# Three edits to the background schedule of an attention + two-MoE-layer kernel on one core: wider spacing of dependent pieces, rounded weights kept in their raw-word buffer, another rhythm for attention

## The chip, the core and the metric

One core of a Trainium2 chip runs the whole program. The metric is device time in microseconds (us) of one launch, measured for whole executions. A profile is one further execution, taken by the hardware profiler; its own time and span stand in the table below.

## What is computed

```python
# windowed attention: 4 x 8 heads, 768 positions, 64 wide; chunks of 32 with 16 left, 8 right, 8 memory slots
scores = scale * np.matmul(q_c, k_full.transpose(0, 1, 3, 2))
a = np.exp(scores - np.max(scores, axis=-1, keepdims=True))
a = a / (np.sum(a, axis=-1, keepdims=True) + 1e-09)
out[:, :, c_start:c_end] = np.matmul(a, v_full)
# x: 3072 tokens x 512; two dense "MoE" layers, 512 -> 2048 -> 512
h = x @ w_in;  r = np.maximum(h, 0.0);  x = (r * r) @ w_out            # first layer
h = x @ w_in;  g = h * np.tanh(softplus(h));  out = g @ w_out          # second layer
```

The four weight matrices arrive as 64-bit floats. The kernel decodes them on the chip into 32-bit floats.

## The kernel before

**Steps and points.** The two layers are worked in 48 steps: layer, then one of three token blocks of 1024 tokens (`sb`), then one of eight slices of d_ff (`j`). Layer 1 is steps 0 to 23, layer 2 steps 24 to 47. In a step PE does seven block products of a Strassen-Winograd scheme for the first matmul of that step (`product`, L527), and, between them, the second matmul of the step before (`unit`, L582, eight units). Each product or unit ends with a call of `rest()`, and that call is a *point*: 15 points in a step, numbered 0 to 14. A full step without attention is 90 matmuls of 128x512.

**What is hung on the points.** `beside` holds, by step and point, everything that is not the main chain: `at(s, i, work)` puts it there, and `rest()` does it. In order of program each point first flushes stores and raw loads that were put off by `later`, then streams one or two weight pieces (`stream_w`, L259: `w1s` for the next step, and in steps 8 to 23 `w2s` for the units of the next step, at points 1, 4, 7 and 10), then does the hung work. Each engine runs its instructions in the order in which they were written, and so does SP, which issues every DMA of this kernel.

**Weights.** `order_w` lists 32 weight blocks (layer, slice, which matrix). For each, `plan_w(s, i, e, order, ...)` hangs nine pieces from point `i` of step `s` on, one letter each; `|` goes on by a point. `A` (ACT, L155) rebuilds the high word into `val`, `D` (DVE, L160 and L163) clips and shifts it, `d` (DVE, L169) joins the low word, `S` and `s` (DVE, L180 to L185) make sums, `R` and `r` (ACT, L207 or L225) round the first and the second part to the fp32r format of the matmuls, `L` and `l` (DVE, L213 or L232) take what the rounding left. The 64-bit words lie in `raws`, two slots used in turn; `load_raw(n + 2)` refills a slot for the block after next. Layer 1's blocks are decoded in steps 0 to 7, two a step; layer 2's 16 blocks one a step in steps 8 to 14 and then one every 10 points from step 17 on. Layer 2's parts are stored to DRAM (`w_d`) and streamed back later.

**Attention.** Group `p` (0 to 11) is 256 tokens by 8 heads. Groups 0 to 3 are done ahead of step 0; groups 4 to 7 are hung from step 0 on and 8 to 11 from step 8 on, by `plan_attention`: scores on PE (L375), maxima on DVE, 16 exponentials on ACT (L411), normalisation (L421, L425), transposes (L433), a copy (`pt`, L443), the product with v (L455), a copy to `stage` (L467), sums on GpSimd, a store. PSUM banks 6 and 7 serve scores, transposes and values of all these groups in turn. `v` of a group shares its buffer (`at1`) with `stage` of the one before, `q` shares `xt0` with the probabilities, and `load_x` reuses `xt0` to `xt2` and `at0`, `at1` in steps 7 and 15 to fetch the next token block, which `split_x` (L287, L289) rounds.

Of the kernel before, what the change touches and what calls it, by code (L numbers as in the profile page):

```python
# [29 lines left out]
NQ = KF // 2  # L30
# [28 lines left out]
def tile_chunk_attention_moe_moe2(  # L59
# [105 lines left out]
    def decode(e):  # L165
        n = order_w.index(e)
        vb = val_t[e][:, 0:1024].bitcast(U32).rearrange("p (h f) -> p h f", h=2)
        low = raw_of(n).bitcast(U32).rearrange("p h (f b) -> p h f b", b=2)[:, :, :, 0]
        nc.vector.scalar_tensor_tensor(  # L169
            out=vb, in0=low, scalar=29, in1=vb, op0=ALU.logical_shift_right, op1=ALU.bitwise_or  # L170
        )
        load_raw(n + 2)

    def sums_w(e, half):

# [41 lines left out]
            del val_t[e]  # L217
            later((w1_d, w2_d)[kind][0][j], w.bitcast(FP32))

    def round_w2(e, i, tag):  # L220

        v0, o, n = parts(e)[i]
        flush()
        hi_t[e, i] = pool.tile([128, 1024], FP32R, tag=tag, name="hi")
        nc.scalar.copy(out=hi_t[e, i][:, 0:n], in_=val_t[e][:, v0:v0 + n])  # L225

    def split_w2(e, i):
        _, j, kind = e
# [453 lines left out]
    def plan_attention(s, i, p):  # L682

        for n, work in {
            0: lambda: scores(p),
            1: lambda: softmax(p, 0),
            2: lambda: softmax(p, 1),
            3: lambda: (exps(p, 0, slice(0, 4)), load_k(p + 1) if (p + 1) % PSB else None),
            4: lambda: exps(p, 0, slice(4, 8)),
            5: lambda: exps(p, 1, slice(0, 4)),  # L690
            6: lambda: exps(p, 1, slice(4, 8)),
            7: lambda: normalize(p),
            8: lambda: load_v(p) if p > PSB else None,
            13: lambda: transpose_p(p),
            14: lambda: (copy_pt(p), load_q(p + 1) if (p + 1) % PSB else None),
            17: lambda: values(p),
            18: lambda: copy_x(p),
            19: lambda: sums_x(p, nc.gpsimd),
            24: lambda: store_x(p),
        }.items():  # L700
            at(s, i + n, work)

# [175 lines left out]
    with tc.manual_schedule():  # L878
# [85 lines left out]

        for s in range(NQ):
            if s + 1 < NQ:
                plan_w(s, 0, (0, s + 1, 0), "A||D|d|RS|s||rL||l", round_w, split_w, "val")
                plan_w(s, 5, (0, s, 1), "A||D|d||R||L", round_w, split_w, "xt2")
            else:
                plan_w(s, 5, (0, s, 1), "A||D|d||R||L", round_w, split_w, "val")  # L970

        seconds = [e for e in order_w if e[0]]
        for n, e in enumerate(seconds):
            if n < NQ - 1:
                plan_w(NQ + n, 3, e, "A||D|d|RS|s|L||||r|l", lambda e, i: round_w2(e, i, "xt2"), split_w2, "val")
            else:
                n -= NQ - 1
                hi = (["xt0", "xt1"], ["xt2", "at1"])[n % 2]
                plan_w(
                    2 * NQ + 1, 10 * n, e, "A||D|d|RS|s|Lr||l",  # L980
                    lambda e, i, hi=hi: round_w2(e, i, hi[i]), split_w2, ("val", "at0")[n % 2],
                )

        for sb in range(NSB - 1):
            p = PSB * (sb + 1)
            start, first, period = sb * NQ, 10, 22
            at(start, 0, lambda p=p: load_q(p))
            if sb:
                at(start, 1, lambda p=p: load_k(p))
# [106 lines left out]
```

## Time and profile before

| what | value |
|---|---|
| time, median of 3 runs (lowest, highest) | 1093.74 us (1091.49, 1094.07) |
| the profiled execution: its own time, its span | 1093.48 us, 1091.7 us |
| PE busy | 1047.6 us, 96% of the span |
| DVE, ACT, GpSimd busy | 76%, 53%, 39% |
| mean granted TensorE clock | 0.987 |
| DMA moved | 321.37 MB, mean 294 GB/s |

The span runs from the first to the last instruction; the time is 1.8 us longer. "PE" is the matmul row, "PEld" the weight loads that run beside it. In the rows further down, "<-" behind an idle time names what ended the wait, and L527 is a line of the kernel as printed above.

### The profile page before, as it was taken

The numbers are of one execution on the slowest core, as the hardware profiler recorded it, in microseconds if no ns is written. First come the engines' busy times: TensorE is split into PE (matmuls) and PEld (weight loads), VectorE is DVE, ScalarE is ACT, GpSimd is POOL, SyncE is SP. The second block draws the span as 40 slices with busy tenths as digits, with TensorE's granted clock in tenths as the row PEclk, the third lists the DMA queues.
The fourth block names the chain that finished last, engine by engine and source line by source line (L and its number), as shares of the span: only waits on it lengthen the run. The fifth ranks groups of instructions, "written<-read, shape, count | busy, mean of one in ns | idle before, by whom it ended". The sixth has DMA issues, their size and how long they took to land.

```text
span 1091.7 us, 19711 instructions
## 1 busy us (share of the span) xinstructions
PE 1047.6 (96%) x7443; PEld 847.9 (78%) x7443; DVE 831.3 (76%) x1027; ACT 583.2 (53%) x1087; POOL 426.5 (39%) x327
## 2 busy tenths in 40 slices
PE   6879999998989999999999999999999999999998
PEld 3557777776778888788888788888888888888887
DVE  5777868759847667778898767887868878867777
ACT  2567765746665764666565654444354443453332
POOL 2224253322324343222222244545455454644443
PEclk9899999999999999999999999999999999999999
DMA  9646867669999998989998988899998899987452
GB/s 352 265 147 252 326 248 267 245 250 345 339 350 342 344 316 289 305 299 361 369 331 318 316 295 283 307 329 320 387 356 279 297 310 360 377 264 228 157 174 77
DMA packets 192142, 321.37 MB, mean 294 GB/s; under 512 B 13488, under 2 KB 151088, under 8 KB 188208
## 3 DMA queue, kind: packets, MB, share of 16 engines
q1 hardware_dynamic: 192048, 320.11, 84.1%
q8 instruction: 60, 0.98, 0.4%
q14 instruction: 34, 0.28, 0.1%
HBM read 228.04 MB, written 92.01 MB: 293 GB/s over the span
## 4 chain that ended last, share of the span: by engine, by line
PE 70%; DVE 11%; DMA 10%; ACT 5%; issue 3%; SPq 1%; DVEq 0%; ACTq 0%
PE banks L527 32%; PE banks L617 20%; PE banks L582 13%; DMA w1s<-w_d 3%; DMA xt_d<-stage 2%; DMA xt<-xt_d 2%; PE banks L455 2%; DVE val L169 2%; DVE y L596 1%; DVE w1s L213 1%; PE banks L375 1%; PE banks L660 1%; ACT p L411 1%; DVE val L163 1%; ACT val L155 1%
## 5 line engine op out<-in xcount | busy, mean ns | idle before, releaser
L527 PE MATMUL banks<-x,w1s 128*128 128x512 f32 x2016 | 496.9, 393 | 12.7 <-DVE u L849 5.3
L527 PEld LDWEIGHTS banks<-x,w1s 128*128 128x128 f32 x2016 | 379.2, 189 | 97.2 <-DVE u L849 6.6
L541 POOL TENSOR_TENSOR g<-r,g 128x512 fp32r<-128x512 f32 x190 | 266.5, 1410 | 478.0 <-ACT g L540 380.3
L582 PE MATMUL banks<-g,w2s 128*128 128x512 f32 x1152 | 282.0, 395 | 7.8 <-DVE y L596 5.7
L582 PEld LDWEIGHTS banks<-g,w2s 128*128 128x128 f32 x1152 | 215.8, 189 | 59.5 <-DVE y L596 9.2
L617 PE MATMUL banks<-g,w2s 128*128 128x512 f32 x828 | 206.5, 389 | 0.0
L617 PEld LDWEIGHTS banks<-g,w2s 128*128 128x128 f32 x828 | 155.4, 188 | 32.4
L540 ACT CAST g<-r 128x512 fp32r<-128x512 f32 x190 | 116.0, 622 | 27.7 <-DVE r L568 23.3
L596 DVE TENSOR_TENSOR y<-banks,y 128x512 f32<-128x512 f32 x168 | 112.0, 680 | 21.4 <-PE banks L582 21.3
L605 DVE TENSOR_TENSOR m<-banks,m 128x1024 f32<-128x1024 f32 (+1 forms) x84 | 101.1, 1209 | 12.4 <-PE banks L617 7.2
L541 POOL TENSOR_TENSOR g<-raws,g 128x512 fp32r<-128x512 f32 x47 | 66.8, 1426 | 62.7 <-ACT g L540 37.2
L546 ACT ACTIVATE r<-r 128x512 f32<-128x512 f32 x72 | 45.5, 632 | 71.0 <-DVE r L857 49.7
L550 ACT ACTIVATE r<-r 128x512 f32<-128x512 f32 x48 | 30.4, 633 | 73.1 <-DVE r L857 37.3
L605 DVE TENSOR_TENSOR raws<-banks,raws 128x1024 f32<-128x1024 f32 x40 | 48.9, 1222 | 26.7 <-PE banks L617 26.7
L547 ACT ACTIVATE r<-r 128x512 f32<-128x512 f32 x96 | 60.9, 634 | 3.1
L232 DVE TENSOR_TENSOR val<-val,hi 128x1024 f32<-128x1024 f32 (+1 forms) x32 | 39.9, 1248 | 29.3 <-ACT hi L225 28.6
L830 DVE TENSOR_TENSOR u<-banks,u 128x512 f32<-128x512 f32 x48 | 32.9, 685 | 26.6 <-ACT u L823 21.8
L849 DVE TENSOR_TENSOR u<-banks,u 128x512 f32<-128x512 f32 x48 | 33.1, 689 | 22.8 <-PE banks L527 20.1
L823 ACT COPY u<-banks 128x512 f32<-128x512 f32 x48 | 28.5, 594 | 39.8 <-PE banks L527 39.7
L169 DVE SCALAR_TENSOR_TENSOR val<-raws,val 128x1024 uint32<-128x1024 uint32 x32 | 48.4, 1511 | 0.7
L425 POOL TENSOR_TENSOR p<-p,sum 128x512 f32<-128x512 f32 x22 | 27.7, 1278 | 52.6 <-DVE sum L422 22.2
L155 ACT ACTIVATE val<-raws 128x1024 f32<-128x1024 f32 x32 | 36.6, 1143 | 21.1 <-DMA w_d<-val 10.1
(96 smaller groups left out, 1078.8 us busy)
## 6 DMA issues: line engine op xcount, KB each, us to landing
w1s<-w_d SPq DMA_DIRECT2D x280, 256.0 KB, 6.0
w2s<-w_d SPq DMA_DIRECT2D x229, 256.0 KB, 6.0
raws<-w_dram SPq DMA_DIRECT2D x64, 512.0 KB, 5.2
w_d<-w1s SPq DMA_DIRECT2D x8, 1792.0 KB, 9.4
x<-xs_d SPq DMA_DIRECT2D x14, 1024.0 KB, 11.3
v<-v_dram SPq DMA_DIRECT2D x24, 512.0 KB, 7.7
xt<-xt_d SPq DMA_DIRECT2D x21, 512.0 KB, 7.7
k<-k_dram SPq DMA_DIRECT2D x24, 368.0 KB, 7.4
```

What stands on the lines that cost most here:

```text
L155: nc.scalar.activation(out=val, in_=high, func=ACTF.Prelu, scale=REBIAS, alpha=NEGATIVE)
L169: nc.vector.scalar_tensor_tensor(out=vb, in0=low, scalar=29, in1=vb, op0=ALU.logical_shift_right, op1=ALU.bitwise_or)
L232: nc.vector.tensor_tensor(out=val, in0=val, in1=hi, op=ALU.subtract)
L527: nc.tensor.matmul(out=ps, lhsT=w[:, a, f:f + 128], rhs=x[:, xi, c, kk, :], start=start and i == 0, stop=stop and i == len(order) - 1, ski ...
L540: nc.scalar.copy(out=g[:, 0], in_=r)
L541: nc.gpsimd.tensor_tensor(out=g[:, 1], in0=r, in1=g[:, 0].bitcast(FP32), op=ALU.subtract)
L546: nc.scalar.activation(out=r, in_=h, func=ACTF.Relu)
L547: nc.scalar.activation(out=r, in_=r, func=ACTF.Square)
L582: nc.tensor.matmul(out=ps, lhsT=w[:, a, blk(f), d % 2 * 128:d % 2 * 128 + 128], rhs=g_t[s, (f, t)][:, c, :], start=i == 0, stop=i == len(o ...
L596: nc.vector.tensor_tensor(out=y, in0=ps, in1=y, op=ALU.add)
L605: engine.tensor_tensor(out=to, in0=in0, in1=in1, op=ALU.add)
L617: nc.tensor.matmul(out=bank(first + d), lhsT=w[:, a, 128 * d:128 * d + 128], rhs=g[:, c, :], start=i == 0 and blk not in ONTO, stop=i == 2 ...
```

## The change

Three things. The order strings of `plan_w` put the pieces of one weight block at other points. For layer 2, the rounded part is no longer written to a buffer of its own (`xt2`, or `xt0`, `xt1`, `at1` in steps 17 on) but over the block's raw words in `raws`; so the refill of that slot can no longer be asked for when the words have been joined (`decode`), and is asked for behind the last store instead (`split_w2`). Attention's groups 4 to 7 begin at point 14 of step 0 instead of point 10, both sets of groups come every 20 points instead of 22, and from the transposes on each piece stands one point earlier in its group (the store two).

```diff
@@ decode
-        load_raw(n + 2)
+        if e[0] == 0:
+            load_raw(n + 2)
@@
-    def round_w2(e, i, tag):
+    def round_w2(e, i):
         v0, o, n = parts(e)[i]
-        flush()
-        hi_t[e, i] = pool.tile([128, 1024], FP32R, tag=tag, name="hi")
+        hi_t[e, i] = raw_of(order_w.index(e))[:, i].bitcast(FP32R)
         nc.scalar.copy(out=hi_t[e, i][:, 0:n], in_=val_t[e][:, v0:v0 + n])
@@ split_w2
         later(d[:, 0, o:o + n], hi)
         later(d[:, 1, o:o + n], val)
         if i == len(parts(e)) - 1:
             del val_t[e]
+            load_raw(order_w.index(e) + 2)
@@ plan_attention
-            13: lambda: transpose_p(p),
-            14: lambda: (copy_pt(p), load_q(p + 1) if (p + 1) % PSB else None),
-            17: lambda: values(p),
+            12: lambda: transpose_p(p),
+            13: lambda: (copy_pt(p), load_q(p + 1) if (p + 1) % PSB else None),
+            16: lambda: values(p),
...
@@ steps 0 to 7
-                plan_w(s, 0, (0, s + 1, 0), "A||D|d|RS|s||rL||l", round_w, split_w, "val")
-                plan_w(s, 5, (0, s, 1), "A||D|d||R||L", round_w, split_w, "xt2")
+                plan_w(s, 0, (0, s + 1, 0), "A||D|d||S|R|s|L|r||l", round_w, split_w, "val")
+                plan_w(s, 4, (0, s, 1), "A||D|||d|||R|||L", round_w, split_w, "xt2")
...
@@ steps 8 to 14, then from step 17
-                plan_w(NQ + n, 3, e, "A||D|d|RS|s|L||||r|l", lambda e, i: round_w2(e, i, "xt2"), split_w2, "val")
+                plan_w(NQ + n, 3, e, "A|D|d|S|Rs||Lr||l", round_w2, split_w2, "val")
...
-                    2 * NQ + 1, 10 * n, e, "A||D|d|RS|s|Lr||l",
+                plan_w(2 * NQ + 1, 10 * n, e, "A||D|d|S|Rs||Lr||l", round_w2, split_w2, ("val", "at0")[n % 2])
...
-            start, first, period = sb * NQ, 10, 22
+            start, first, period = sb * NQ, (14, 10)[sb], 20
```

Most line numbers of the kernel after (L173 to L221, and L238 to the plan at L979) are higher by one than here: its L260 is L259 here, its L850 is L849.

SP in step 19, points 6 to 10, before (`hi` is the rounded part, `val` what is left; what an instruction waits for stands in brackets, and `DMAHW` is a semaphore that counts landed DMAs):

```order
L136 DMA w_d<-hi 128x768 [waits DMAHW3_49,Activation_49]
L136 DMA w_d<-val 128x768 [waits DMAHW4_49,DVE_49]
L259 DMA w2s<-w_d 128x2x256 [waits DMAHW5_49]
L259 DMA w1s<-w_d 128x2x256 [waits DMAHW6_49]
L136 DMA w_d<-hi 128x1024 [waits DMAHW7_49,Activation_49]
L136 DMA w_d<-val 128x1024 [waits DMAHW0_49,DVE_49]
L259 DMA w1s<-w_d 128x2x256 [waits DMAHW1_49]
L259 DMA w2s<-w_d 128x2x256 [waits DMAHW2_49]
```

and the same place after:

```order
L136 DMA w_d<-raws 128x768 [waits DMAHW2_49,Activation_49]
L136 DMA w_d<-val 128x768 [waits DMAHW3_49,DVE_49]
L260 DMA w1s<-w_d 128x2x256 [waits DMAHW4_49]
L136 DMA w_d<-raws 128x1024 [waits DMAHW5_49,Activation_49]
L136 DMA w_d<-val 128x1024 [waits DMAHW6_49,DVE_49]
L136 DMA raws<-w_dram 128x1024 [waits DMAHW7_49,DMAHW2_49]
L136 DMA raws<-w_dram 128x1024 [waits DMAHW5_49,DMAHW0_49]
L260 DMA w1s<-w_d 128x2x256 [waits DMAHW1_49]
L260 DMA w2s<-w_d 128x2x256
```

Between the store of the second rounded part and the `w2s` piece of point 10 there now stand two refills of `raws`, and the second of them waits for DMAHW5, which is that store's own landing. It is so again in steps 17 and 21; elsewhere the refills come at other points.

DVE in step 2, around point 6 and 7, before (L849 makes `u` of the chain, which the product at point 10 waits for; the first L213 takes what rounding left of `w1s`):

```order
L185 TENSOR_TENSOR val<-val 128x256
L849 TENSOR_TENSOR u_1528<-banks,u_1380 128x512
L851 TENSOR_TENSOR r<-banks,u_1528 128x512
L213 TENSOR_TENSOR w1s<-val,w1s 128x768
L160 TENSOR_SCALAR val<-val 128x1024
L163 TENSOR_SCALAR val<-val 128x1024
L596 TENSOR_TENSOR y<-banks,y 128x512
L169 SCALAR_TENSOR_TENSOR val<-raws,val 128x1024
```

and after:

```order
L160 TENSOR_SCALAR val<-val 128x1024
L163 TENSOR_SCALAR val<-val 128x1024
L394 TENSOR_REDUCE mx<-banks 128x8
L401 TENSOR_SCALAR mneg<-mx 128x8
L850 TENSOR_TENSOR u_1518<-banks,u_1373 128x512
L852 TENSOR_TENSOR r<-banks,u_1518 128x512
L186 TENSOR_TENSOR val<-val 128x256
L597 TENSOR_TENSOR y<-banks,y 128x512
L214 TENSOR_TENSOR w1s<-val,w1s 128x768
```

The pair L160, L163 of the second weight block has moved ahead of L849, the sum L185 and the take-off L213 behind it.

ACT at the turn from step 0 to step 1, before (L823 copies the bank that the product of point 5 adds to; L411 are the exponentials of group 4):

```order
L411 ACTIVATE p,sum<-banks,mneg 128x64 x8
L155 ACTIVATE val<-raws 128x1024
L411 ACTIVATE p,sum<-banks,mneg 128x64 x4
L823 COPY u_1128<-banks 128x512
L411 ACTIVATE p,sum<-banks,mneg 128x64 x4
```

and after:

```order
L155 ACTIVATE val<-raws 128x1024
L824 COPY u_1109<-banks 128x512
L412 ACTIVATE p,sum<-banks,mneg 128x64 x8
L595 COPY y<-banks 128x512
L155 ACTIVATE val<-raws 128x1024
```

All exponentials of group 4 now stand behind that copy.

## Rows read from the trace of the kernel before

**Rows 1.** Busy time by stretch (windows): steps 0-7, 8-10, 11-15, 17-23; PEclk granted clock.

```profile
57.00:257.83 200.83, 182.93 (x1734) 145.98 (x1733) 151.95 (x202) 130.48 (x292) 68.46 (x54) 0.97 0.71 257
257.83:334.49 76.66, 70.86 (x667) 56.90 (x666) 55.50 (x78) 51.23 (x130) 23.96 (x20) 0.98 0.98 348
334.49:450.49 116.00, 115.58 (x1117) 94.84 (x1116) 79.58 (x111) 68.81 (x156) 44.26 (x36) 1.00 0.94 321
472.74:616.56 143.82, 143.31 (x632) 118.10 (x630) 123.24 (x162) 84.79 (x125) 38.01 (x27) 1.00 0.97 343
```

**Rows 2.** Waits of PE from 57 to 450 us: total, times, longest.

```profile
PE banks L527 <- DVE u L849: 5.3, 3, 3.3
PE banks L582 <- DVE y L596: 4.6, 6, 2.0
PE banks L527 <- ACT u L823: 4.4, 2, 3.1
PE banks L363 <- ACT stage L467: 3.0, 2, 2.8
PE banks L455 <- ACT val L155: 1.8, 1, 1.8
```

**Rows 3.** Waits of PE from 472 to 616 us.

```profile
PE banks L582 <- DMA w2s<-w_d: 0.4, 1, 0.4
```

**Rows 4.** Windows: a stretch at low granted clock, and step 19 whole.

```profile
83.90:87.30 3.40, 3.40 (x10) 2.61 (x9) 3.29 (x6) 1.54 (x5) 1.74 (x2) 0.50 0.71 284
514.20:534.60 20.40, 20.40 (x91) 16.89 (x90) 18.51 (x26) 14.81 (x22) 7.24 (x5) 1.00 1.00 361
```

**Rows 5.** Timeline of PE, steps 0 and 1: start, length, idle before.

```profile
66.22 1.66 PE L527 MATMUL banks<-x,w1s 128*128 128x512 f32 x6 [1.57 <-DVE u L849]
...
74.17 3.01 PE L527 MATMUL banks<-x,w1s 128*128 128x512 f32 x12 [1.93 <-DVE r L857]
...
82.97 1.29 PE L527 MATMUL banks<-x,w1s 128*128 128x512 f32 x4 [3.07 <-ACT u L823]
```

**Rows 6.** Timeline of DVE in step 0.

```profile
67.67 0.69 DVE L160 TENSOR_SCALAR val<-val 128x1024 f32<-128x1024 f32 x1
...
70.09 2.20 DVE L169 SCALAR_TENSOR_TENSOR val<-raws,val 128x1024 uint32<-128x1024 uint32 x1
72.21 1.21 DVE L213 TENSOR_TENSOR w1s<-val,w1s 128x1024 fp32r<-128x1024 f32 x1
```

**Rows 7.** Timeline of SP at the turn to step 7.

```profile
228.34 0.38 SPq L481 DMA_DIRECT2D xt_d<-stage  x1
...
239.98 1.21 SPq L273 DMA_DIRECT2D xt<-xt_d  x2
```

**Rows 8.** Timeline of ACT in step 7.

```profile
244.57 1.05 ACT L287 CAST x<-xt 128x1024 fp32r<-128x1024 f32 x1 [11.15 <-DMA xt<-xt_d]
```

**Rows 9.** Timeline of ACT in step 10.

```profile
312.99 1.05 ACT L225 CAST hi<-val 128x1024 fp32r<-128x1024 f32 x1 [3.68 <-DMA w_d<-hi]
313.94 1.06 ACT L467 COPY stage<-banks 128x512 f32<-128x512 f32 x2
```

**Rows 10.** Timeline of ACT in step 19.

```profile
528.76 0.62 ACT L540 CAST g<-r 128x512 fp32r<-128x512 f32 x1
```

**Rows 11.** Timeline of SP in step 19.

```profile
530.72 1.03 SPq L259 DMA_DIRECT2D w2s<-w_d  x1
```

**Rows 12.** Timeline of PE at point 3 of step 20.

```profile
538.68 1.52 PE L582 MATMUL banks<-g,w2s 128*128 128x512 f32 x6
```

**Rows 13.** Stores of `hi`, 472 to 600 us, from issue to landing.

```profile
DMA to landing us min/median/max: 2.6/6.1/8.0
```

**Rows 14.** Weight pieces (L259), 472.7 to 596 us, from issue to landing.

```profile
DMA to landing us min/median/max: 5.2/6.7/8.1
```

**Rows 15.** DMA issues of the whole run: size of one, median us to landing.

```profile
v<-v_dram SPq DMA_DIRECT2D x24, 512.0 KB, 7.7
...
w_d<-hi SPq DMA_DIRECT2D x17, 512.0 KB, 4.7
```

More of the change, by code (lines that the diff above doesn't have):

```diff
@@ L693, in plan_attention @@
             8: lambda: load_v(p) if p > PSB else None,
-            13: lambda: transpose_p(p),
-            14: lambda: (copy_pt(p), load_q(p + 1) if (p + 1) % PSB else None),
-            17: lambda: values(p),
-            18: lambda: copy_x(p),
-            19: lambda: sums_x(p, nc.gpsimd),
-            24: lambda: store_x(p),
+            12: lambda: transpose_p(p),
+            13: lambda: (copy_pt(p), load_q(p + 1) if (p + 1) % PSB else None),
+            16: lambda: values(p),
+            17: lambda: copy_x(p),
+            18: lambda: sums_x(p, nc.gpsimd),
+            22: lambda: store_x(p),
         }.items():
@@ L966, in tile_chunk_attention_moe_moe2 @@
             if s + 1 < NQ:
-                plan_w(s, 0, (0, s + 1, 0), "A||D|d|RS|s||rL||l", round_w, split_w, "val")
-                plan_w(s, 5, (0, s, 1), "A||D|d||R||L", round_w, split_w, "xt2")
+                plan_w(s, 0, (0, s + 1, 0), "A||D|d||S|R|s|L|r||l", round_w, split_w, "val")
+                plan_w(s, 4, (0, s, 1), "A||D|||d|||R|||L", round_w, split_w, "xt2")
             else:
-                plan_w(s, 5, (0, s, 1), "A||D|d||R||L", round_w, split_w, "val")
+                plan_w(s, 4, (0, s, 1), "A||D|||d|||R|||L", round_w, split_w, "val")
         seconds = [e for e in order_w if e[0]]
@@ L974, in tile_chunk_attention_moe_moe2 @@
             if n < NQ - 1:
-                plan_w(NQ + n, 3, e, "A||D|d|RS|s|L||||r|l", lambda e, i: round_w2(e, i, "xt2"), split_w2, "val")
+                plan_w(NQ + n, 3, e, "A|D|d|S|Rs||Lr||l", round_w2, split_w2, "val")
             else:
                 n -= NQ - 1
-                hi = (["xt0", "xt1"], ["xt2", "at1"])[n % 2]
-                plan_w(
-                    2 * NQ + 1, 10 * n, e, "A||D|d|RS|s|Lr||l",
-                    lambda e, i, hi=hi: round_w2(e, i, hi[i]), split_w2, ("val", "at0")[n % 2],
-                )
+                plan_w(2 * NQ + 1, 10 * n, e, "A||D|d|S|Rs||Lr||l", round_w2, split_w2, ("val", "at0")[n % 2])
         for sb in range(NSB - 1):
             p = PSB * (sb + 1)
-            start, first, period = sb * NQ, 10, 22
+            start, first, period = sb * NQ, (14, 10)[sb], 20
             at(start, 0, lambda p=p: load_q(p))
```

## The prediction

> **What bounds the kernel now.** I read the stage table first. PE does the work that ends last: it is busy for 96% of the span, and a full step without attention takes 20.40 us with PE busy in all of it [rows 4]. So time can only be won where PE waits or runs slowly, and the table says where. From step 11 to 15 PE lacks 0.4 us of 116.0, in steps 17 to 23 0.5 us of 143.8. In steps 0 to 7 it lacks 17.9 us of 200.8, in steps 8 to 10 5.8 us of 76.7 [rows 1]: 23.7 us together. The list of PE's waits says for whom: mostly DVE (`u`, `y`, `r`) and ACT (`u`, `stage`) [rows 2]. One of them, the 1.8 us put down to ACT `val`, was over for ACT's part, since that instruction stands behind the waiting one in the program; the load of `v` is what was late there.
>
> Second, the clock. A wait of 3.07 us [rows 5] is followed by 3.4 us at a granted clock of 0.50, which is 1.2 GHz [rows 4], and costs 1.7 us again. Waits of 1.57 and 1.93 us were not followed by one [rows 5]. There are five such stretches between 57 and 335 us, 8.5 us. With the idle time that is 32.2 us at most to win, all of it before 335 us.
>
> Third, the DMA queue. DMA is at a share of 0.98 in steps 8 to 10 and 0.97 in steps 17 to 23 [rows 1]. SP issues in order and waits itself: the load of `xt` at 239.98 stood for some 11 us after the store of 228.34, which writes what it reads, and held all that SP had behind it [rows 7]. The one DMA wait of PE in steps 17 to 23, 0.4 us, is for `w2s` [rows 3]: these pieces arrive with nothing to spare.
>
> **The change part by part.** The number of instructions and bytes is the same; all the cost is in waiting. My unit is the point, 20.40/15 = 1.36 us.
>
> *Steps 0 to 2.* The exponentials of group 4 now stand behind ACT's copy `u`, so the wait of 3.07 us goes and its slow stretch with it: 4.8 us. The wait of 1.93 us came from a join (2.20) and a take-off (1.21) on DVE just ahead of `r` [rows 5, 6]; these now stand elsewhere: 1.9 us. Against that, a pair of 0.69 each takes the place of a shorter sum ahead of L849 [rows 6], so the 1.57 becomes about 2.6: 1.0 lost. And three new waits: the second matmul of step 1 needs the `w2s` take-off, which moved from point 12 to point 0 of step 1, behind two activations and a cast; the transposes of group 4 need a normalisation behind a late GpSimd operation; the values at point 0 of step 2 need the copy `pt`, hung at point 12, ACT's fullest point. I put each at 1.2 to 1.5 us by adding ACT's durations from the end of step 0: 3.9 lost. Net gain 1.8.
>
> *Steps 3 to 6.* The wait for `v` (1.8 and a slow stretch) shrinks: the `w2s` store that shared the DMA engines with it is issued later. Gain 3.0. The waits for `y` [rows 2] in step 5, 2.4 us with a slow stretch, come from DVE's backlog after point 7, which the spacing spreads into points 6 and 0, where DVE had nothing: gain 3.6, less 1.0 for the values at point 0 of step 6. Net 2.6. If DVE stays behind there, both stay.
>
> *Step 7.* Group 7's store moves from point 10 to point 6 of step 6, 5.4 us earlier and ahead of the big weight store. The load of `xt` then needn't wait; it can land near 239 us, where the rounding of `x` began only at 244.57 [rows 7, 8]. PE's 3.3 us for `u` [rows 2], the following 0.8 and 1.2 us for `y` and the slow stretch, 7.0 us, shrink to about 1. Gain 6.0.
>
> *Steps 8 to 10.* The rounded part no longer shares one buffer for both halves, so ACT no longer stands 3.68 us for a landing ahead of the copies to `stage` [rows 9]. That was the longest wait of L363 [rows 2], 3.0 with its tail, plus a slow stretch. Gain 4.7.
>
> *Steps 10 to 14.* `q` and `v` of groups 10 and 11 are now issued just behind a refill of `raws` that waits for a store's landing, and 8 points ahead of use instead of 9. A load of `v` takes 7.7 us in the median [rows 15]; with the hold before it that is a point too late at three or four places: 3.5 lost. The bounds are 0 and 10 (each wait 2.5).
>
> Sum to here: 1.8 + 3.0 + 2.6 + 6.0 + 4.7 - 3.5 = 14.6 us won; bounds 5 (the new waits twice as long) and 25 (none of them).
>
> *Steps 17 to 22.* Here the refill stands directly ahead of the `w2s` piece of point 10 in steps 17, 19 and 21. Step 19 worked out: the second rounding follows the activation group that ended at 529.38 [rows 10] and takes 1.05; DVE frees that group 0.9 sooner, so the store goes at 529.5. It lands in 4.7 us (this size, whole run [rows 15]) to 6.1 (this stretch [rows 13]); I take 5.4: 534.9. Then the refill and a `w1s` piece are issued, 1.0 us, and the `w2s` piece goes at 535.9 instead of 530.72 [rows 11]. With 6.7 us [rows 14] it lands at 542.6. PE comes to it with its third matmul after 538.68 [rows 12], at 539.1. So PE waits 3.5 us, and by what the waits above did, a slow stretch follows, 1.7. Three times: 15.6 us lost. Nothing covers it: PE has 0.5 us to spare in the whole stretch [rows 1]. Bounds: 2.6 and 5.2 us [rows 13, 14] give no wait; 8.0 and 8.1 give 7.5 each, 27.6 in all.
>
> The Trainium skill, "DMA: Bandwidth & Descriptors", section "Anatomy of one DMA — SWDGE (gpsimd) path", gives 2.0 us plus the bytes at 436 GB/s for a DMA, a fit for the GpSimd path. By that, as an estimate, the store would take 3.2 us and the piece 2.6; the piece would land at 536.3, the loss would be zero and the time 1079. The trace has 4.7 to 6.7 us for these two [rows 13 to 15], on SP's queue with others in flight, so the page's price is not used; it speaks for the first rival.
>
> Sum: the profiled execution took 1093.48 us (the median of the three is 1093.74). 1093.5 - 14.6 + 15.6 = 1094.5. I say 1094.
>
> **The rivals.**
>
> *The holds stay hidden (0.26).* If the store lands within 3.5 us and the piece within 5.2, it arrives at 539.2, when PE comes. For it: with SP held, less is in flight than in the rows. Against: the pieces' least time was 5.2 with the queue as it is. Then 1093.5 - 14.6 = 1079.
>
> *ACT stays behind in the opening (0.20).* The copies `pt` of groups 4 and 7 stand behind two gates and a cast, 1.9 + 1.9 + 1.05 = 4.9 us, with three points, 4.1 us, until the values. If ACT enters point 11 of steps 1 and 5 more than 2 us late, each of these two waits grows from about 1.2 to 2.8 and draws a slow stretch: 6.6 us of the gain gone, 1101. ACT is busy for 65% of steps 0 to 7 [rows 1], which speaks against; groups of 16 exponentials in four points speak for.
>
> *Attention's loads are late (0.12).* Groups every 20 points ask for a tenth more in steps 8 to 13, with DMA at 0.98 [rows 1]. If the four waits of steps 10 to 14 are 2.5 us and two draw a slow stretch, that is 13.4 instead of 3.5: 1104.
>
> *Nothing moves (0.04).* The waits only change their names: 1093.5.
>
> **How the numbers follow.** My forecast, both the gain and the holds, has 0.38 and by itself a range of 1088 to 1100. A difference under 0.3%, 3.3 us, can't be told from none here. The forecast gives 0.08 faster, 0.18 the same and 0.12 slower; the first rival is faster, the second and third slower, the last the same. So faster 0.34, same 0.22, slower 0.44. The range, 1081 to 1108, leaves out the best part of the first rival and the upper bound of the holds.
>
> **What would show it.** Right: in PE's waits, L528 for `u` of ACT near 80 us gone; step 7's wait under 1.5 us; waits of L583 for `w2s` at point 3 of steps 18, 20 and 22, 2 to 5 us each, with a granted clock of 0.50 behind them; on SP, refills of `raws` that stand for 4 to 6 us ahead of a `w2s` piece. Wrong: no wait for `w2s` after 472 us (first rival); values in steps 2 and 6 waiting over 2 us for `pt` (second); values or scores in steps 10 to 13 waiting for loads (third). The prediction fails worst if gain and holds miss on the same side.

## The result: 1.3% slower, and where the profile after puts it

The kernel after took 1107.37 us (median of 4 runs, 1104.01 to 1109.06), the kernel before 1092.62 us beside it (4 runs, 1091.13 to 1094.07). The ratio is 1.0131, with a 95% interval of 1.0102 to 1.0161. The prediction said 1094 with a range of 1081 to 1108 and gave slower 0.44: the range held the time, and the forecast itself was 13 us too low. The profiled execution of after took 1106.99 us, its span is 1105.2 us, its mean granted clock 0.981 (before 0.987). DMA moved the same 321.37 MB.

The stage table of after, cut at the same steps as that of before [rows 1] (bounds, length, busy time of PE, PEld, DVE, ACT and GpSimd, granted clock, DMA share, GB/s):

```profile
56.70:251.71 195.01, 182.69 (x1735) 147.29 (x1733) 153.44 (x202) 129.49 (x291) 70.59 (x54) 0.96 0.71 259
251.71:333.66 81.95, 74.00 (x675) 60.35 (x674) 57.71 (x79) 55.13 (x134) 26.02 (x21) 0.94 0.94 334
333.66:451.98 118.32, 115.08 (x1109) 94.05 (x1108) 76.20 (x110) 66.64 (x152) 38.98 (x35) 1.00 0.93 319
474.26:627.83 153.57, 145.31 (x632) 118.99 (x630) 123.53 (x161) 84.38 (x124) 36.02 (x27) 0.99 0.91 320
```

The bounds are the starts of steps 0, 8, 11, 16, and of 17 and 24, so they can be read as a clock. Step 8 begins 6.1 us earlier than before (251.71 against 257.83), step 11 only 0.8 us earlier, step 16 begins 1.5 us later, and so does step 17. Steps 17 to 23 take 153.57 us instead of 143.82, 9.8 us more. Some 2 us more come later, in steps that no part of the change touches. So the gain that the prediction put ahead of step 17, 14.6 us, is not there: 6.1 us of it came by step 8, 5.3 of these were given back in steps 8 to 10, and the rest, with 1.5 us more, in steps 11 to 15.

The list of PE's waits from 56 to 452 us (total, times, longest):

```profile
PE banks L434 <- POOL p L426: 4.8, 5, 1.8
PE banks L583 <- DVE w2s L214: 4.2, 2, 3.4
PE banks L528 <- DVE u L850: 4.0, 2, 3.4
PE banks L456 <- DMA v<-v_dram: 2.8, 2, 2.0
PE banks L456 <- ACT pt L444: 2.6, 4, 1.6
PE banks L376 <- DMA q<-q_dram: 1.8, 1, 1.8
PE banks L583 <- ACT w2s L208: 1.7, 1, 1.7
```

and from 472 to 628 us:

```profile
PE banks L583 <- DMA w2s<-w_d: 7.8, 3, 3.3
```

Beside [rows 2] nearly every name is new. The waits for ACT's `u` (4.4 us) and for `stage` (3.0) are gone or under a microsecond, that for `y` fell from 4.6 to 0.8 in this list. In their place stand the transposes behind GpSimd's normalisation, two waits for pieces of `w2s`, `v`, `q` and `pt`. The 7.8 us for `w2s` behind step 17 stood at 0.4 before [rows 3].

**The hold in steps 17 to 22.** SP in step 19 and PE at point 3 of step 20 (timeline):

```profile
533.00 0.32 SPq L136 DMA_DIRECT2D w_d<-raws  x1
...
535.19 3.75 SPq L136 DMA_DIRECT2D raws<-w_dram  x2
...
539.57 0.60 SPq L260 DMA_DIRECT2D w2s<-w_d  x1
...
544.90 3.93 PE L583 MATMUL banks<-g,w2s 128*128 128x512 f32 x10 [2.40 <-DMA w2s<-w_d]
```

Two refills need some 0.7 us to be issued; here they need 3.75 because the second one stands until the store of 533.00 has landed, at 538.5. Behind them the `w2s` piece goes at 539.57, and PE stands 2.40 us for it. In steps 17 and 21 the refills stand for 3.62 and 3.64 us, and PE for 2.07 and 3.30 us in the step behind. This is the mechanism as it was predicted, at its three places.

**The loss at step 8.** ACT, DVE and PE in steps 7 and 8 (timeline):

```profile
251.93 0.63 ACT L547 ACTIVATE r<-r 128x512 f32<-128x512 f32 x1 [4.07 <-DVE r L858]
...
256.58 1.04 ACT L208 CAST w2s<-val 128x1024 fp32r<-128x1024 f32 x1
...
260.34 1.22 DVE L214 TENSOR_TENSOR w2s<-val,w2s 128x1024 fp32r<-128x1024 f32 x1
...
257.67 0.50 PE L583 MATMUL banks<-g,w2s 128*128 128x512 f32 x1 [1.72 <-ACT w2s L208]
261.62 2.93 PE L583 MATMUL banks<-g,w2s 128*128 128x512 f32 x6 [3.44 <-DVE w2s L214]
```

The new string puts the rounding of the last `w2s` block at point 12 of step 7 and its take-off at point 0 of step 8. ACT stood idle for 4.07 us ahead of the gates of points 11 and 12, and the rounding stands behind both of them; the take-off stands behind `y`. PE waits 5.2 us for these two, and six matmuls in 2.93 us instead of 1.52 [rows 12] show the low clock behind.

**GpSimd.** In step 3 (timeline):

```profile
124.38 1.28 POOL L542 TENSOR_TENSOR g<-r,g 128x512 fp32r<-128x512 f32 x1 [6.24 <-DMA raws<-w_dram]
125.62 2.04 POOL L426 TENSOR_TENSOR p<-p,sum 128x512 f32<-128x512 f32 x2
...
126.72 0.66 PE L434 MATMUL banks<-cst,p 128*128 128x128 f32 x4 [1.76 <-POOL p L426]
```

Group 5's normalisation now stands behind a gate's operation on GpSimd, ahead of which it stood before, and the transposes want its result a point earlier.

### The profile page after: what moved, and what is told of

Read it like the earlier page. It is cut to its first block, busy times and chain, and to the rows that moved or that the text cites. A ratio compares the mean times of both kernels' runs of the same rounds, so it can differ in the third digit from the quotient of the medians.

```text
span 1105.2 us, 19712 instructions
## 1 busy us (share of the span) xinstructions
PE 1052.6 (95%) x7443; PEld 852.6 (77%) x7443; DVE 832.9 (75%) x1027; ACT 583.4 (53%) x1087; POOL 423.5 (38%) x327
## 2 busy tenths in 40 slices
DMA packets 192142, 321.37 MB, mean 291 GB/s; under 512 B 13488, under 2 KB 151088, under 8 KB 188208
## 5 line engine op out<-in xcount | busy, mean ns | idle before, releaser
L542 POOL TENSOR_TENSOR g<-r,g 128x512 fp32r<-128x512 f32 x190 | 263.6, 1394 | 513.4 <-ACT g L541 421.5
L232 DVE TENSOR_TENSOR val<-val,raws 128x1024 f32<-128x1024 f32 (+1 forms) x32 | 41.1, 1284 | 18.5 <-ACT raws L225 18.5
L169 DVE SCALAR_TENSOR_TENSOR val<-raws,val 128x1024 uint32<-128x1024 uint32 x32 | 52.1, 1629 | 0.4
L831 DVE TENSOR_TENSOR u<-banks,u 128x512 f32<-128x512 f32 x48 | 32.9, 685 | 21.4 <-PE banks L528 21.3
L850 DVE TENSOR_TENSOR u<-banks,u 128x512 f32<-128x512 f32 x48 | 32.9, 686 | 16.8 <-PE banks L528 13.9
L547 ACT ACTIVATE r<-banks 128x512 f32<-128x512 f32 x24 | 14.4, 602 | 58.1 <-PE banks L528 58.0
L290 DVE TENSOR_TENSOR x<-xt,x 128x1024 fp32r<-128x1024 f32 x21 | 28.3, 1345 | 19.9 <-ACT x L288 19.4
```

Source lines behind the costliest of these rows:

```text
L169: nc.vector.scalar_tensor_tensor(out=vb, in0=low, scalar=29, in1=vb, op0=ALU.logical_shift_right, op1=ALU.bitwise_or)
L542: nc.gpsimd.tensor_tensor(out=g[:, 1], in0=r, in1=g[:, 0].bitcast(FP32), op=ALU.subtract)
L547: nc.scalar.activation(out=r, in_=h, func=ACTF.Relu)
L831: nc.vector.tensor_tensor(out=u2, in0=b, in1=u1, op=ALU.add)
```

## The experiments

The table gives for each kernel the median time, its ratio to the kernel before beside it with the 95% interval, and the length of each stretch in the profile, from PE's first product of one step to that of another. One stretch of unchanged code differs between two executions: steps 0 to 6 took 172.5, 173.7, 173.7 and 170.9 us in four kernels that are alike there (after, own17, step7_back, refill_4_later).

| run | us | ratio (interval) | 0-6 | 7-8 | 9-11 | 12-14 | 15-16 | 17-23 |
|---|---|---|---|---|---|---|---|---|
| before | 1092.62 | 1 | 173.5 | 51.3 | 77.8 | 69.3 | 43.8 | 143.8 |
| after | 1107.37 | 1.0131 (1.0102-1.0161) | 172.5 | 51.7 | 78.9 | 71.1 | 43.4 | 153.6 |
| own17 | 1099.95 | 1.0057 (1.0036-1.0078) | 173.7 | 53.3 | 78.6 | 71.1 | 43.1 | 147.7 |
| refill_4_later | 1096.61 | 1.0026 (1.0011-1.0042) | 170.9 | 52.6 | 75.0 | 74.8 | 43.3 | 145.8 |
| step7_back | 1104.94 | 1.0100 (1.0082-1.0118) | 173.7 | 47.8 | 80.6 | 71.1 | 43.2 | 154.5 |
| offsets_back | 1098.65 | 1.0048 (1.0031-1.0064) | 166.1 | 50.9 | 80.7 | 69.3 | 42.9 | 153.8 |
| l1_alone | 1091.88 | 0.9984 (0.9968-1.0000) | 168.7 | 56.0 | 76.0 | 69.4 | 44.2 | 144.4 |
| att_alone | 1098.32 | 1.0044 (1.0029-1.0060) | 176.7 | 50.1 | 77.6 | 71.6 | 41.9 | 144.4 |
| l2_alone | 1115.62 | 1.0190 (1.0168-1.0213) | 175.0 | 51.0 | 78.8 | 72.7 | 45.9 | 158.0 |
| hi_over_raws | 1105.83 | 1.0109 (1.0090-1.0128) | 174.8 | 52.3 | 78.8 | 69.1 | 47.2 | 150.6 |
| l1_steps1to6 | 1087.43 | 0.9946 (0.9932-0.9959) | 167.9 | 49.9 | 79.0 | 69.4 | 43.9 | 143.5 |
| l1_and_raws_8to14 | 1086.16 | 0.9929 (0.9912-0.9946) | 166.3 | 50.2 | 74.7 | 69.7 | 45.8 | 143.7 |
| three_mended | 1084.36 | 0.9911 (0.9892-0.9931) | 166.5 | 45.8 | 77.2 | 72.2 | 45.4 | 145.2 |
| parts_kept | 1079.06 | 0.9858 (0.9837-0.9879) | 168.2 | 44.9 | 74.8 | 69.3 | 46.6 | 143.2 |

### The holds: own17 and refill_4_later

own17 gives the rounded parts buffers of their own again from step 17 on:

```diff
@@ decode
-        if e[0] == 0:
+        if e[0] == 0 or n > 22:
             load_raw(n + 2)
... (round_w2 takes the buffer; split_w2 asks for a refill only for blocks up to 22)
@@ from step 17 on
-                plan_w(2 * NQ + 1, 10 * n, e, "A||D|d|S|Rs||Lr||l", round_w2, split_w2, ("val", "at0")[n % 2])
+                hi = (["xt0", "xt1"], ["xt2", "at1"])[n % 2]
+                plan_w(2 * NQ + 1, 10 * n, e, "A||D|d|S|Rs||Lr||l",
+                    lambda e, i, hi=hi: round_w2(e, i, hi[i]), split_w2, ("val", "at0")[n % 2])
```

> The kernel after, but from step 17 on the rounded parts again have buffers of their own (xt0, xt1, xt2, at1) and the refill of raws is asked for when the words are joined; order strings and points stay as after. Theory (the holds: a refill that waits for a store's landing stands ahead of the w2s piece of point 10): the waits of PE for w2s in steps 18, 20, 22 and 24 (8.1 us together) go, steps 17 to 23 take 143.8 us as before instead of 153.6, the time is 1097 to 1099. Rival (the pieces arrive late anyway, by the queue's load or the new order of the pieces): w2s waits of 2 us or more stay in at least two of these steps and the time is 1104 or more.

Measured: 1099.95 us, 0.74 points of the ratio less than after. Steps 17 to 23 take 147.7 us. PE's waits from 472 to 624 us (L588 is the line of the units here):

```profile
PE banks L588 <- DMA w2s<-w_d: 3.3, 3, 1.3
```

Most of the 7.8 us is gone, about 1 us a place is left, where 143.8 us had been expected. So some 6 us of the 9.8 hang on the refill. The other 4 stay with the new order strings, which this kernel keeps: in step 19 the second half of the block is stored 16.3 us after the step began instead of 14.2, and the `w2s` piece of point 10, which stands behind that store on SP, goes at 18.6 us, against 16.5 before and 22.2 in after. Whether it was the place on SP or the shared buffer remained to be told; refill_4_later keeps the shared buffer and asks for the refill later:

```diff
@@ split_w2
-            load_raw(order_w.index(e) + 2)
@@ plan_w
         for n, names in enumerate(order.split("|")):
             at(s, i + n, *(work[name] for name in names))
+        if e[0]:
+            at(s, i + n + 4, lambda: load_raw(order_w.index(e) + 2))
```

> The kernel after, with layer 2's refill of raws asked for four points (5.4 us) later, when the rounded part's store has landed; the rounded parts stay over the raw words, nothing else is changed. Theory (the cost is SP standing for the landing ahead of the w2s piece, not the shared place of rounded part and raw words): waits for w2s in steps 18, 20 and 22 of about 1 us as with buffers of their own from step 17 on, where 7.4 us were won, and the waits for q in step 11 (1.8) and v in step 9 (2.8 with its tail) shrink too: 1095 to 1099. Rival (the pieces are late by the new order of stores and the load of the queue): waits for w2s of 2 us or more stay, 1103 or more.

Measured: 1096.61 us, 1.05 points less than after, the largest gain of a single edit to it. SP in step 19, and PE's waits from 472 to 620 us:

```profile
532.39 1.01 SPq L259 DMA_DIRECT2D w2s<-w_d  x1
...
534.11 3.17 SPq L136 DMA_DIRECT2D raws<-w_dram  x2
```

```profile
PE banks L582 <- DMA w2s<-w_d: 1.7, 2, 1.3
```

The refills still stand on SP for 3.17 us, but behind the `w2s` piece. That settles it: the shared place costs little, the position of a DMA that waits ahead of one that is wanted costs the time. Steps 17 to 23 take 145.8 us with the new order strings, so these cost 2 us here and 4 in own17.

Steps 9 to 11 fell to 75.0 us as well, and the wait for `q` in step 11 is gone: in after `q` is issued at 339.99, behind a refill that could go only at 338.19; here it goes at 330.65, ahead of the refill. The wait for `v` in step 9 is another matter. It shrank from 2.8 to 0.9 us (with 1.2 for ACT beside it), but it is not a refill that holds this load. SP in step 9 of after:

```profile
287.95 0.42 SPq L136 DMA_DIRECT2D xt_d<-ty  x1
...
296.42 0.81 SPq L346 DMA_DIRECT2D v<-v_dram  x2
```

`ty` holds differences of the first token block's result (`plan_sums`) and shares the buffer `at1` with `v`; its store landed at 296.35, and the load went right then. Before it was so too (295.70 and 295.76). And what steps 9 to 11 gained, steps 12 to 14 lost: they take 74.8 us instead of 71.1, with a wait of 2.6 us for GpSimd's normalisation in step 12 and a slow stretch, the reason of which was not followed.

### Step 7's block: step7_back

```diff
-                plan_w(s, 4, (0, s, 1), "A||D|||d|||R|||L", round_w, split_w, "val")
+                plan_w(s, 5, (0, s, 1), "A||D|d||R||L", round_w, split_w, "val")
```

> The kernel after, with the w2s block of step 7 alone back on its points of before (rounding at point 10, take-off at point 12). Theory: its rounding stands ahead of ACT's gate of point 11 again, where ACT waited 4.07 us for DVE, so the waits of 1.72 and 3.44 us at point 3 of step 8 and half of the slow stretch of 3.4 us go, step 9 begins 6 to 7 us earlier and the time is 1100 to 1102. Rival (DVE and ACT have too much in step 7 wherever it stands): PE waits for u or y in step 7 instead, the time stays at 1105 or more.

Measured: 1104.94 us, 0.31 points less than after, 2.4 us; the intervals of the two ratios overlap. ACT in step 7:

```profile
248.65 1.05 ACT L208 CAST w2s<-val 128x1024 fp32r<-128x1024 f32 x1
252.72 0.63 ACT L547 ACTIVATE r<-r 128x512 f32<-128x512 f32 x1 [3.02 <-DVE r L858]
```

The rounding lies in ACT's idle time again and the two waits at step 8 are gone: steps 7 and 8 take 3.9 us less, against 6 to 7 expected, in part because a wait of 1.2 us for `y` stands there now. Neither theory gave 2.4: the place was right, and in this profile 1.7 us came back in steps 9 to 11, where PE waits for `v` and for `q` as in after, and 0.9 in steps 17 to 23.

### Attention: offsets_back and att_alone

```diff
-            12: lambda: transpose_p(p),
-            13: lambda: (copy_pt(p), load_q(p + 1) if (p + 1) % PSB else None),
-            16: lambda: values(p),
-            17: lambda: copy_x(p),
-            18: lambda: sums_x(p, nc.gpsimd),
+            13: lambda: transpose_p(p),
+            14: lambda: (copy_pt(p), load_q(p + 1) if (p + 1) % PSB else None),
+            17: lambda: values(p),
+            18: lambda: copy_x(p),
+            19: lambda: sums_x(p, nc.gpsimd),
```

> The kernel after, with the transposes, pt, values, stage copy and sums of each group one point later, as before (store and start stay). Theory: the waits of the transposes for the normalisation on GpSimd (1.3, 2.1 and 1.4 us in steps 1, 3, 12) and those of the values for pt in step 4 (1.8) shrink by 1.36 us each and a slow stretch goes with one or two: 1100 to 1104. Rival (GpSimd and ACT are later by as much, since they stand behind the same gates): 1105 to 1109.

Measured: 1098.65 us, 0.83 points less than after, more than either theory had. No wait of a transpose for GpSimd is left, the values wait 0.4 us for `pt`, and steps 0 to 6 take 166.1 us instead of 172.5. The difference lies in steps 2 to 6 (125.2 us instead of 131.4), and most of it is the clock: after has 10.2 us at the low clock there, 6.8 of them behind the wait for `pt` in step 4, and this kernel none. So a point of slack for waits of 1 to 2 us was worth 4.5 to 6 us there (own17, step7_back and refill_4_later, alike with after in these steps, took 129.7 to 129.9). In steps 9 to 11 the kernel gives 1.8 us back, with a wait of 4.2 us for `q` in step 11. att_alone makes attention's part of the change on the kernel before (start, period and offsets, as in the diff of the change):

> The kernel before with attention's start, period and offsets alone changed. By the prediction's terms: 4.8 in step 1 and 6.0 in step 7 are won, 3.5 lost in steps 10 to 14: 1085, with step 8 beginning about 9 us earlier than before (257.8). Rival, from the trace of after: the gain up to step 8 comes, but waits for v, for q and for the normalisation on GpSimd in steps 3, 9, 11 and 12 and a long stretch at 1.2 GHz give 6 or more back: 1089 to 1094, with step 15 beginning no more than 3 us earlier than before (429.0).

Measured: 1098.32 us, which neither theory had: slower than before, and already by step 7 (176.7 against 173.5 us). PE's waits from 56 to 450 us, the ACT row in step 7, and SP ahead of it:

```profile
PE banks L433 <- POOL p L425: 7.1, 9, 1.6
PE banks L455 <- ACT pt L443: 6.7, 8, 2.1
```

```profile
234.49 0.33 SPq L136 DMA_DIRECT2D w_d<-w2s  x1
...
236.16 2.72 SPq L273 DMA_DIRECT2D xt<-xt_d  x2
...
246.53 1.05 ACT L287 CAST x<-xt 128x1024 fp32r<-128x1024 f32 x1 [9.47 <-DMA xt<-xt_d]
```

The two waits of the earlier pieces come to 13.8 us. And the gain of step 7 is not there: `xt` is asked for without standing, 15 us after the store that it reads (220.84), but 1.7 us behind a big `w2s` store, and lands some 10 us later. In after the new string of layer 1 puts that store behind the first `xt` load, and the load of 230.31 was used at 238.94. The gain of step 7 needed both edits (26.5 us here, 26.9 in l1_alone, 22.6 in after); the prediction gave it to the earlier store alone.

### Layer 1's strings: l1_alone and l1_steps1to6

l1_alone has the two strings of steps 0 to 7 as after (see the diff of the change); l1_steps1to6 leaves steps 0 and 7 as before:

```diff
+                one, start, two = ("A||D|d||S|R|s|L|r||l", 4, "A||D|||d|||R|||L") if s else ("A||D|d|RS|s||rL||l", 5, "A||D|d||R||L")
-                plan_w(s, 0, (0, s + 1, 0), "A||D|d|RS|s||rL||l", round_w, split_w, "val")
-                plan_w(s, 5, (0, s, 1), "A||D|d||R||L", round_w, split_w, "xt2")
+                plan_w(s, 0, (0, s + 1, 0), one, round_w, split_w, "val")
+                plan_w(s, start, (0, s, 1), two, round_w, split_w, "xt2")
```

> The kernel before with the two order strings of steps 0 to 7 alone changed. By the prediction's terms: the wait for r at point 1 of step 1 (1.9) and those for y in step 5 (3.6 with the slow stretch) go, 1.3 is lost in step 1: about 1088. Rival, from the trace of after: the rounding of the last w2s block at point 12 of step 7 stands behind ACT's gate and its take-off at point 0 of step 8 behind DVE's y, so PE waits 3 to 5 us at point 3 of step 8 and a stretch at 1.2 GHz follows: 1092 to 1096.

> The kernel before with layer 1's new order strings in steps 1 to 6 alone; steps 0 and 7 keep the strings of before. Theory: the strings' gain lies in steps 2 to 6 (120.7 us there with the strings alone, 129.1 before), their losses in steps 0 and 1 (u behind the clipping pair, 3.4 us) and at step 8 (w2s, 5.1 us and a slow stretch): this keeps the gain without the losses, 1083 to 1087. Rival (the gain in steps 2 to 6 hangs on what steps 0 and 1 leave behind): 1089 to 1092.

Measured: 1091.88 us, no difference that can be told and at the lower end of the rival, and 1087.43 us, faster by 0.54% and just above the upper end of the theory. In l1_alone PE's waits from 252 to 270 us are the two of after:

```profile
PE banks L582 <- DVE w2s L213: 3.4, 1, 3.4
PE banks L582 <- ACT w2s L207: 1.6, 1, 1.6
```

Without them steps 7 and 8 take 49.9 instead of 56.0 us. Steps 2 to 6 take 120.7 us in the one and 120.6 in the other, 129.1 before (128.2 and 128.3 in hi_over_raws and l2_alone, alike with before there): that is the spacing's gain, some 8 us, and it hangs neither on step 0 nor on step 7.

### Layer 2's part: l2_alone, hi_over_raws, l1_and_raws_8to14

l2_alone has all of layer 2's part; hi_over_raws has it without its strings; both on the kernel before:

```diff
@@ hi_over_raws: decode, round_w2 and split_w2 as after, also from step 17 on, and
-                plan_w(NQ + n, 3, e, "A||D|d|RS|s|L||||r|l", lambda e, i: round_w2(e, i, "xt2"), split_w2, "val")
+                plan_w(NQ + n, 3, e, "A||D|d|RS|s|L||||r|l", round_w2, split_w2, "val")
```

> The kernel before with layer 2's part alone changed (rounded parts over the raw words, refill behind the last store, the two order strings from step 8 on). By the prediction's terms: 4.7 won in steps 8 to 10, 15.6 lost in steps 17 to 22: 1103. Theory after the trace of after: the same gain, holds of 9.5 in all: 1097. Rival (the gain of steps 8 to 10 is not there): step 11 begins at 334 as before and the time is 1101 to 1103.

> The kernel before, in which the rounded parts of layer 2 are written over the raw words and the refill comes behind the last store; the order strings are those of before. Theory (the strings of layer 2 bunch the pieces at points 7 to 11 and cost most of what that part cost alone, 20 us; the refill stands a point earlier than with the new strings, so a hold costs 2.6 less 1.4): waits for w2s of 1 to 2 us in steps 18, 20 and 22, no wait for stage in step 10, time 1093 to 1099. Rival (the refill that waits for a landing, standing on SP, costs most, also in steps 9 to 15 where it holds loads of q, v and xt): PE waits for loads or for what hangs on them in steps 9 to 15, time 1105 or more.

Measured: 1115.62 and 1105.83 us. For both the rival came closer than the theory, and l2_alone is slower than any number that was put down. By itself this part loses more (1.9%) than the whole change. SP at the turn to step 15 of l2_alone, and ACT and PE behind it:

```profile
433.32 0.38 SPq L136 DMA_DIRECT2D w_d<-raws  x1
...
435.01 5.05 SPq L136 DMA_DIRECT2D raws<-w_dram  x2
...
441.40 0.56 SPq L274 DMA_DIRECT2D xt<-xt_d  x1
...
447.87 1.04 ACT L288 CAST x<-xt 128x1024 fp32r<-128x1024 f32 x1 [11.26 <-DMA xt<-xt_d]
...
450.83 1.65 PE L528 MATMUL banks<-x,w1s 128*128 128x512 f32 x3 [2.61 <-DVE u L850]
```

It is the hold again, now ahead of `xt`: the refills stand for 5.05 us and PE's `u` is late by 2.61 in step 15 (by 3.9 in hi_over_raws), where 0.4 stood before. In hi_over_raws the last take-off is a point earlier from step 17 on, and the waits for `w2s` are 5.4 us in all instead of 8.0. PE's waits of hi_over_raws from 280 to 640 us:

```profile
PE banks L583 <- DMA w2s<-w_d: 5.4, 3, 2.1
PE banks L528 <- DVE u L850: 3.9, 1, 3.9
...
PE banks L456 <- DMA v<-v_dram: 2.5, 1, 2.5
```

The wait for `stage` in step 10 is gone, as predicted, and one for `v` in step 9 has its place. What the new strings add in steps 12 to 14 of l2_alone (72.7 against 69.1 us) was not followed further. l1_and_raws_8to14 takes the hold out: l1_steps1to6, the rounded parts over the raw words in steps 8 to 14, the refill four points late, strings as before.

```diff
@@ decode
-        load_raw(n + 2)
+        if e[0] == 0 or n > 22:
+            load_raw(n + 2)
... (round_w2 without a buffer in steps 8 to 14; layer 1 as in l1_steps1to6)
@@ plan_w
+        if e[0] and order_w.index(e) <= 22:
+            at(s, i + n + 4, lambda: load_raw(order_w.index(e) + 2))
```

> The kernel before with layer 1's new strings in steps 1 to 6 (1087.4 by itself) and, in steps 8 to 14 alone, the rounded parts over the raw words with the refill four points behind the last take-off; layer 2's strings and the buffers from step 17 on as before. Theory (the prediction's gain of 4.7 us in steps 8 to 10 is there once no refill stands for a landing): no wait for stage in step 10 (2.6) and no slow stretch there, no new wait for v or q, 1082 to 1085. Rival (the gain isn't there: another wait takes the place of that for stage): 1086 to 1089.

Measured: 1086.16 us, 0.17 points under l1_steps1to6, too little to tell the two apart, and by its time the rival's. But the profile shows the prediction's term: steps 9 to 11 take 74.7 us instead of 79.0, and 4.1 us of the difference lie in step 10, where the wait for `stage` stood. PE's waits there (250 to 340 us) in l1_steps1to6,

```profile
PE banks L363 <- ACT stage L467: 2.6, 2, 2.4
PE banks L582 <- ACT y L594: 2.1, 1, 2.1
```

and in l1_and_raws_8to14:

```profile
PE banks L459 <- DMA v<-v_dram: 1.5, 1, 1.5
```

1.9 us of it are given back in steps 15 and 16 (`w2s`, 3.2 us at point 3 of step 16), where the refill asked for at the end of step 14 is now issued among the loads of `xt`.

### Put together: three_mended and parts_kept

three_mended is after with the edits of refill_4_later, offsets_back and step7_back. parts_kept is the kernel before with the edits that gained: those of l1_and_raws_8to14, but step 14's block as before, and groups 4 to 7 from point 14 every 20 points with the offsets of before.

```diff
@@ parts_kept, beside l1_and_raws_8to14 (with 21 for 22)
+                hi = "xt2" if n == 6 else None
-                plan_w(NQ + n, 3, e, "A||D|d|RS|s|L||||r|l", round_w2, split_w2, "val")
+                plan_w(NQ + n, 3, e, "A||D|d|RS|s|L||||r|l", lambda e, i, hi=hi: round_w2(e, i, hi), split_w2, "val")
...
-            24: lambda: store_x(p),
+            22: lambda: store_x(p),
...
-            start, first, period = sb * NQ, 10, 22
+            start, first, period = sb * NQ, (14, 10)[sb], (20, 22)[sb]
```

> The kernel after with three things at once: the refill of raws four points later, attention's transposes to sums one point later, and the w2s block of step 7 on its points of before. Theory (these three are the loss and act in stretches of their own): stretch by stretch, taking for each the run that mended it (41.1 us for steps 0 and 1, 125.2 for 2 to 6, 47.8 for 7 and 8, 75.0 for 9 to 11, 69.3 for 12 to 14, 145.8 for 17 to 23, the rest as after), the time is 1080 to 1084. Rival (mended in one stretch they come back in the next, as the 3.9 us of step 7 did in steps 9 to 11): 1086 or more.

> The kernel before with what gained alone: layer 1's new strings in steps 1 to 6; the rounded parts over the raw words in steps 8 to 13 with the refill four points late, step 14 as before; groups 4 to 7 from point 14 every 20 points with the offsets of before and the store two points earlier. Layer 2's strings, the buffers from step 14 on and groups 8 to 11 as before. Theory: the gains of the single runs add by stretch (about 41 us for steps 0 and 1, 125 for 2 to 6 with the work of group 4 moved there, 48 for 7 and 8, 75 for 9 to 11, the rest as before), 1078 to 1082. Rival (attention's later start gives nothing beside the new strings): 1084 to 1087, as with the strings and the rounded parts alone.

Measured: 1084.36 us (1080.54 to 1086.31) and 1079.06 us (1074.85 to 1082.03), the first 0.4 us above the range of its theory, the second within it. The three mends alone turn 1.3% slower into 0.9% faster, 23.0 us, about the sum of their single gains (10.8, 8.7 and 2.4 us). parts_kept beats both kernels, by 1.4% (0.9858, interval 0.9837 to 0.9879) and by 28 us. Its stage table, cut as above:

```profile
57.66:246.83 189.17, 178.30 (x1734) 142.83 (x1734) 157.74 (x205) 130.34 (x292) 68.04 (x54) 0.99 0.73 268
246.83:320.45 73.62, 70.40 (x667) 57.20 (x666) 55.34 (x78) 50.33 (x129) 23.94 (x20) 0.98 0.98 356
320.45:437.21 116.76, 115.40 (x1118) 95.06 (x1116) 78.03 (x112) 69.49 (x156) 44.20 (x36) 1.00 0.95 329
461.58:604.74 143.16, 143.16 (x632) 118.02 (x630) 122.97 (x162) 84.57 (x125) 38.07 (x27) 1.00 0.97 345
```

Against [rows 1] the first stretch is 11.7 us shorter and the second 3.0; steps 17 to 23 have no idle time of PE. Steps 15 and 16 are 2.8 us longer, with 2.1 us of waits for `w2s`: there is a little left.

## Why the prediction was right and wrong

That the range held the time is luck. The gain fell short by 16.1 us (14.6 forecast, 1.5 lost), the holds cost 5.9 us less than forecast, and 2 us came behind step 24; the sum, some 12 us, left the time 0.6 us inside the upper end, with a gain that lies below the lower bound of 5 us that the working gave it.

**Right: the holds, as a mechanism.** Waits for `w2s` at point 3 of steps 18, 20 and 22, behind a refill that stands on SP, came where the text put them, and taking the refill from ahead of the piece takes them away. Off was the size: 15.6 us predicted, 9.8 measured. In step 19 the store landed in 5.5 us (5.4 taken), and the piece went 22.2 us after the step began, as against 21.7 in the working; but it landed in 5.2 us, not in 6.7. The three waits were 2.07, 2.40 and 3.30 us for 3.5 each, and only one of them drew a slow stretch: 9.5 us. Of the 9.8 us, 2 to 4 go with the new strings, by refill_4_later and own17, and weren't in the working. The first rival, holds that stay hidden, is refuted: it wanted the store to land within 3.5 us. The Trainium skill, "DMA: Bandwidth & Descriptors", section "Anatomy of one DMA — SWDGE (gpsimd) path", spoke for it: its fit, for that path, gives 3.2 and 2.6 us as an estimate. This trace has 5.5 and 5.2 us on SP's queue.

**Wrong: the gain of 14.6 us.** Ahead of step 17 the kernel lost 1.5 us. Its terms one by one:

- *Steps 0 to 2 (1.8).* The waits for ACT's `u` (3.07) and for `r` (1.93) went. The one for DVE's `u` grew to 3.39, not 2.6, and drew 6.8 us of low clock, which was not in the sum. Of the three new waits the transposes' came (1.3); the two others were 0 in this profile. The stretch came out 1.7 us shorter (65.4 us for 67.1), the size of the term, but by luck: own17 and step7_back, alike with after there, took 68.3 us (refill_4_later 65.4).
- *Steps 3 to 6 (5.6).* They came out 0.7 us longer. The waits for `v` and `y` went, and the spacing's gain is real: some 8 us in l1_steps1to6. The step that failed is that the new waits of transposes and values were looked for in groups 4 and 7 alone. A point earlier they stand behind GpSimd's gate operation or ACT's gate in groups 5 and 6 too: 2.1 us in step 3, 1.8 in step 4, each with a slow stretch. offsets_back takes them away, and 4.5 to 6 us of steps 2 to 6 come back.
- *Step 7 (6.0).* It fell by 4.8 us (22.6 against 27.4), and that was given back at point 3 of step 8: the prediction followed what the spacing does at points 6 to 12 of a step, and not what it does where the last take-off falls into the next step and the matmul of point 3 wants it. It had seen this in step 1 and priced it there; and of the 7.0 us that it put into step 7, the wait of 1.2 for `y` stands at that very point of step 8 (263.26).
- *Steps 8 to 10 (4.7).* ACT's wait for a landing went and the `stage` wait with it. What failed is that `v` of group 8, in step 9, was left out: 2.8 us of waits with 6.8 us of low clock, in the place of `stage`. Its load goes when the store of `ty` has landed, as before. But PE now comes to these values, which stand a point earlier, 17.4 us after the step began instead of 20.8, and the load lands at 21.3 instead of 20.2, since that store took 8.4 us instead of 6.3. What made the store slower stays open. With the refill late and attention as before the gain is there, 4.1 us in step 10 of l1_and_raws_8to14.
- *Steps 10 to 14 (loss of 3.5).* 3.2 us of waits came, 1.8 for `q` behind a refill, as worked out, and 1.4 for GpSimd. The size was right, half the cause wasn't.

**The other rivals.** ACT behind in the opening did not come where it was put: the values in step 2 did not wait, those in step 6 waited 0.8 us; its mechanism showed in step 4. Late loads came in steps 9 and 11: 4.6 us, 8.0 with half of the slow stretch, against the 13.4 of that rival. Of the 2 us behind step 24, 0.8 lie in steps 24 and 25 and are there in every kernel that has layer 2's new strings from step 17 on (41.7 to 41.8 us for these two, 41.0 to 41.5 in the others); the rest is 420.8 us from step 26 to 48 in after, 420.1 in step7_back and 419.0 to 419.6 in the twelve other kernels, and what makes it stays open.

## What to carry to other kernels

On an engine or queue that issues in order, look at every wait that an edit adds and list what stands behind it: a buffer that is saved by reuse costs little if its refill is asked for when the last reader is done, and some 10 us here if asked for earlier. Spacing dependent pieces pays until the last piece crosses the place where it is wanted, so check the ends (the first and last step of a loop, the turn to the next one) apart from the middle. When a large change moves the time little, undo its parts one at a time: here a gain of some 14 us (with the refill moved) and a loss of twice that lay in one diff.

## What the runs showed of the hardware

The same wait of PE does not always draw a low clock. Windows of after: at the wait of 3.39 us in step 0, behind that of 1.61 us for `pt` in step 4, then behind those of 2.40 (step 20), 2.07 (step 18) and 3.30 us (step 22); columns as in the stage table:

```profile
66.60:73.40 6.80, 5.66 (x33) 4.04 (x41) 6.47 (x9) 4.71 (x7) 1.43 (x1) 0.50 0.41 141
172.40:179.20 6.80, 6.80 (x101) 5.77 (x94) 3.69 (x5) 3.77 (x8) 1.28 (x1) 0.50 0.62 161
...
544.50:547.90 3.40, 3.00 (x7) 2.45 (x8) 1.24 (x3) 0.96 (x1) 0.00 (x0) 0.50 1.04 369
501.50:504.90 3.40, 3.40 (x15) 2.83 (x16) 2.27 (x3) 0.00 (x0) 0.00 (x0) 1.00 1.06 387
590.70:594.10 3.40, 3.40 (x15) 2.83 (x16) 2.21 (x3) 0.00 (x0) 0.00 (x0) 1.00 1.04 388
```

The wait of 3.30 us was followed by the full clock (2.4 GHz), that of 2.40 us by 3.4 us at a granted 0.50 (1.2 GHz), 15 matmuls in 3.4 us against 7. In l2_alone three waits of 2.72, 2.69 and 2.60 us at the same points drew 3.4, 6.8 and 3.4 us. In before the waits of 1.80 us for `v` in step 3 and of 1.96 for `y` in step 5 drew 3.4 us each, that of 1.93 for `r` none. So the prediction's 1.7 us behind every wait of the holds was wrong in both directions: two of three waits drew nothing in after, and stretches of twice that length occur, three of them between 57 and 628 us of after, where those of before were all 3.4 us. What decides it the runs do not show.
